# A block product of the output done by seven smaller products, GpSimd's work in short pieces, and loads asked for one stage ahead

## The chip, the cores and the metric

The kernel runs on one core of a Trainium2 chip. The core has TensorE (PE, matrix products; PEld is its weight load), VectorE (DVE), ScalarE (ACT), GpSimd (POOL) and the queue of SyncE (SP), from which nearly all transfers are issued. Every engine works through its own list of instructions in order, and semaphores make one engine wait for another. The metric is the device time of one execution in microseconds (us), as the median of several runs.

## The reference

Two stages follow each other. The first is an attention without a softmax over pairs: q is normalised along the head's 64 elements, k along the sequence, and a 64x64 product of k and v for each batch and head is applied to q. The second is a two-layer network with an exact Gelu over all tokens.

```
q_s = exp(q - max) / sum over d          # [8, 8, 576, 64]
k_s = exp(k - max) / sum over s
kv  = einsum('bhsd,bhse->bhde', k_s, v)
x   = einsum('bhsd,bhde->bhse', q_s, kv) -> [4608 tokens, 512]
h   = x @ w_in                           # 512 -> 2048
g   = 0.5 * h * (1 + erf(h / sqrt(2)))
out = g @ w_out                          # 2048 -> 512
```

## The kernel before

The tokens go through in nine chunks of 512. Chunk c = 0 to 7 holds the first 512 positions of batch c; chunk 8 (`B` in the code) holds the remaining 64 positions of all eight batches. All matrix operands are bf16, sums are f32 in the eight banks of PSUM.

**The stages of a chunk.** In the steady part (chunks 3 to 7) TensorE's order is: the first layer of chunk c (`h_waves`), the second layer of chunk c (`y_phase`), and, ahead of that layer's last product, `next_x`: the x of chunk c+1 (`x_all`), the transposing DMA of q for batch c+2 (`xbar_step`), and the k-v product of batch c+2 (`kv_step`). So attention runs two batches ahead of the network's output. The order of everything is written out by hand: the kernel's text is the order on each engine, and a layer beneath it adds the semaphores. `y_phase` takes a table `ins` of functions, and `after(i)` calls those of entry i at that place.

**Seven products instead of eight.** Both layers are 2x2 block products, done with seven products of half size and sums of their operands and results. In the second layer the blocks are 256 tokens by 1024 by 256 columns. Product m is 16 matmuls with a stationary 128x128 block and 256 moving columns (`mm` in `y_phase`, line 691). Product 3 multiplies g[UP, LO], the upper half of g's 1024 rows for the first 256 tokens, by the upper right block of the weights, in which a difference of weights was stored before. Its result goes to the bank `bx` (named yx) and from there to the output's block `c12`. The products' order is 4, 3, 5, 1, 2, 6, then `next_x`, then 7. Products 5, 1 and 2 use sums that VectorE makes in `s_parts` (arrays s5 and s12); 6 and 7 use differences that it makes in place in g (lines 404 and 405).

**Around the change.** At the end of `h_waves` the Gelus of the last quarter tiles (lines 606 and 607) and `s_parts` run on ScalarE and VectorE while TensorE is already in the output phase. In `y_phase`, ScalarE then copies yd (line 706), takes the exponentials of q for batch c+2 (entry 8: a table load and four activations), copies yx (709), takes those of k (entry 9) and copies the second yd (724). VectorE subtracts (716), makes the row sums of q (`q_sums`, in entry 1), and combines results (719, 721, 731). GpSimd first makes a one-element copy that depends on the last in-place difference (`touch_g`, 1086), casts v to bf16 in four pieces (line 190), scales q in one instruction of 2048 elements a partition (`q_scale`, 269), and does the two last combinations of the output on 128x512 f32 tiles (732 and 733). Only then SP can send the first of the two output stores.

**Loads.** `load(nb)` asks for q, k and v of batch nb from SP at the start of chunk c = nb-2's first layer; `load_qrest` does so for chunk 8's q. Each of the three has two buffers. Batches 2 to 4 are loaded earlier. The transposing DMA and the output stores are on the same queue.

In `h_waves`, VectorE's sums that are written r (`r_sum`) and qb (`e_sum`) take a PSUM bank and an SBUF tile or the reverse; TensorE's product 7 of the first layer may write the bank qa only after `e_sum` has read it. `x_sums` makes the operand sums of the first layer (quad_t).

The functions that the change touches, with their callers:

Of the kernel before, what the change touches and what calls it, by code (L numbers as in the profile page):

```python
# [16 lines left out]
def kernel(  # L17
# [70 lines left out]
    HT = M // 2  # L88
    HN = DM // 2
    w7 = singles.tile([128, HK, HN], BF16)  # L90
    s12 = singles.tile([128, HK, M], BF16)
    s5 = singles.tile([128, HK, HT], BF16)

# [10 lines left out]
    def load_main(b, name, t, parts=1):  # L104
# [5 lines left out]
        for i in range(parts):  # L110
            nc.sync.dma_start(out=f[:, i * n:(i + 1) * n, :], in_=src[:, i * n:(i + 1) * n, :])

    def load_pair(b, name, t, parts=1):
        f = f32in.tile([128, HP, NS * D], FP32, tag=name + "f")
        st[b][name + "f"] = f
        src = t[b].rearrange("h (p n) d -> (h p) (n d)", n=NS).rearrange("(x q) f -> q x f", q=128)
        n = HP // parts
        for i in range(parts):
            h0 = i * n
            if b == 0 and name == "k" and i == 0:  # L120

                nc.scalar.dma_start(out=f[:, 0, :], in_=src[:, 0, :])
                h0 = 1
            nc.sync.dma_start(out=f[:, h0:(i + 1) * n, :], in_=src[:, h0:(i + 1) * n, :])
# [8 lines left out]
    def load_v1(i):  # L133

        if i == 0:
            st[1]["vf"] = f32in.tile([128, HP, NS * D], FP32, tag="vf", name="f")
        src = v[1].rearrange("h (p n) d -> (h p) (n d)", n=NS)
        nc.sync.dma_start(out=st[1]["vf"][:, i, :], in_=src[i * 128:(i + 1) * 128, :])

# [52 lines left out]
    def cast_v_all(b):  # L192
        for hp in range(HP):
            cast_v(b, hp, nc.gpsimd)
# [71 lines left out]
    def q_scale(b, eng, i=0, n=1):  # L266
        w = H // n
        e = st[b]["eq"][:, :, i * w:(i + 1) * w, :]
        eng.tensor_tensor(  # L269
            out=e, in0=e, in1=st[b]["recq"].unsqueeze(3).to_broadcast([128, J, w, D]), op=ALU.mult,  # L270
        )

    def norm_q(b, i=0, n=1, eng=None):

# [184 lines left out]
        roles.update(bb=r["x3"], ba=r["kv1"], x0=r["bb"], x1=r["kv0"], x2=r["x0"], x3=r["ba"],  # L459
                     kv0=r["x1"], kv1=r["x2"])  # L460

    def h_waves(c, mid):

# [48 lines left out]
        def r_sum(q):  # L514
            tt(held["r", q], held["A", q], held["r", q])
# [49 lines left out]
        else:  # L565
# [11 lines left out]
            mm(7, 0, 1)  # L577
            r_sum(0)
            r_sum(1)
            mm(3, 0, 1)  # L580
            for q in (2, 3):
                mm(5, q)
# [22 lines left out]
            mm(4, 2, 3)  # L605
        gelu("A", 2, 3)
        gelu("B", 2, 3)
        s_parts(c, 0, 4, (0,))
        if mid:
            s_parts(c, 0, 4, (4,))  # L610
        s_parts(c, 0, 4, (2,))
        s_parts(c, 4, 4, (0,))
        s_parts(c, 4, 4, (3,))
        s_parts(c, 4, 4, (4,))
        turn_roles()
# [54 lines left out]
        }  # L670
        return act, wgt

    def y_phase(c, ins):

# [23 lines left out]
        def after(i):  # L700
            for fn in ins.get(i, []):
                fn()

        mm(4, bd, True)
        if c > 1:
            nc.scalar.copy(out=f, in_=bd)
            after(8)
            mm(3, bx, True)
            nc.scalar.copy(out=c12, in_=two(bx))
            after(9)  # L710
        else:
            nc.vector.tensor_copy(out=f, in_=bd)
        after(0)
        mm(5, be, True)
        after(7)
        tt(f, f, be, ALU.subtract)
# [9 lines left out]
        if c == 1:  # L726
            mm(3, be, False)
            nc.scalar.copy(out=c12, in_=two(be))
        after(4)
        mm(6, bb, True)  # L730
        tt(c22, c22, two(bb))
        tt(c22, c22, c12, eng=nc.gpsimd)
        tt(c22, c22, c21, ALU.subtract, eng=nc.gpsimd)
        after(5)
        mm(7, ba, False)
        tt(c11, two(f), two(ba))
        y_store(c, 1, ysb[1])
        y_store(c, 0, ysb[0])
        after(6)

    def y_last(c):

# [304 lines left out]
    for t in range(4):  # L1047
# [4 lines left out]
    mix_wo(1, 1)  # L1052
    mix_wo(3, 1)
    quad["r"] = wst.tile([128, 4, 2, HT], FP32, tag="w2", name="r")
    quad["t"] = wst.tile([128, 4, 2, HT], BF16, tag="w3", name="quad_t")
    h1 = {p + 3: [lambda p=p: cast_v(2, p, nc.scalar)] for p in range(HP)}
    h1[1] = [sums[0]]
    h1[3] += sums[1:3]
# [3 lines left out]
    exp_q(2, parts=2)  # L1062
    exp_k(2)

    y_phase(1, {
        0: [sums[3]],
        7: [lambda: norm_q(2, 0, 2)],
        1: [lambda: norm_q(2, 1, 2, nc.vector)],
        2: [lambda: cast_v_all(3), lambda: xbar_step(2), lambda: exp_q(3)],
        3: [lambda: kv_step(2), lambda: exp_k(3), lambda: q_sums(3)],  # L1070
        4: [lambda: table(AF.Gelu)],
        6: [lambda: load(4), lambda: x_all(2, (3, 4, 1, 5)),
            lambda: kv_step(3, lambda: x_sums(2, (1,))), lambda: x_sums(2, (2,))],
    })

    def q_late():


        nc.gpsimd.tensor_copy(out=scr[:, 2:3], in_=quad["r"][:, 0, 0, 0:1])
        q_scale(3, nc.gpsimd)  # L1080
        xbar_step(3)

    def touch_g(c):

# [13 lines left out]

    for c in range(2, B + 1):
        nb = c + 2  # L1100
        if 2 < c and nb < B:
            load(nb)
        elif nb == B:
            load_qrest()
        h_waves(c, q_late if c == 2 else None)
        s_parts(c, 4, 4, (2,))
        yi = {}
        if nb <= B:
            yi[8] = [lambda: exp_q(nb)]
            yi[1] = [lambda: norm_q(nb)]  # L1110
            yi[3] = [lambda: table(AF.Gelu)]
        if nb < B:
            yi[9] = [lambda: exp_k(nb)]
            yi[0] = [lambda: touch_g(c), lambda: cast_v_all(nb)]
        if c < B:
            yi[5] = [lambda: next_x(c, nb)]
            y_phase(c, yi)
        else:
            y_last(c)

# [29 lines left out]
```

## Time and profile before

| | us |
|---|---|
| median of 3 runs | 256.49 |
| lowest and highest | 256.13, 256.66 |
| the profiled execution's own time | 256.13 |
| its span on the engines | 254.3 |
| one steady chunk (product 4 at 136.48 to 162.23) | 25.75 |
| TensorE busy | 247.7 |
| VectorE, ScalarE, GpSimd busy | 209.0, 189.1, 67.3 |

The span is what the profile draws, from the first instruction to the last; the run's own time has 1.8 us more around it. A row of a timeline gives the start in us from the span's start, the length in us, the engine, the source line, the operation, output and inputs by the program's names, sizes, and the count that was merged into the row; in brackets stands how long the engine was idle before it and what ended that. Source lines can be those of a helper: 428 is the helper of all tensor-tensor sums, 497 and 694 the matmuls of the two layers. A matmul's length includes its way through the array; the next one starts long before it ends.

### The profile page before, as it was taken

To read this page: it belongs to the slowest core of one execution; us is meant where nothing else is said; L and a number is where in the kernel's file an instruction comes from. 1 tells how busy PE (TensorE), PEld (TensorE's weight loads), DVE (VectorE), ACT (ScalarE), POOL (GpSimd) and SP (SyncE) were. 2 spreads that over 40 slices of the span, in tenths; PEclk is the share of its full clock that TensorE was granted. 3 is DMA by queue.
4 is the path that set the end of the run, shared out by engine and by line. 5 is a ranking of instruction groups with operands and counts; after the bars stand their busy time and mean duration, and the time that the engine had idled before them with its cause. 6 is when DMAs were issued, how large, how long until landed. Compare 5 with 4: busy or idle time off the path is not lost.

```text
span 254.3 us, 6526 instructions
## 1 busy us (share of the span) xinstructions
PE 247.7 (97%) x2672; PEld 195.8 (77%) x2678; DVE 209.0 (82%) x365; ACT 189.1 (74%) x321; POOL 67.3 (26%) x64
## 2 busy tenths in 40 slices
PE   7899999999999999999999999999999999999994
PEld 3444444448888888888888888888888888888883
DVE  1878799888986989897889888988898889578972
ACT  4785988699977995899689968896886787158711
POOL 1530023000735067006700580059000900040000
PEclk9999999999999999999999999999999999999999
DMA  7999999994439935980499049904830340012033
GB/s 237 400 387 425 402 406 400 398 411 174 85 125 330 266 68 131 321 340 1 109 303 377 4 85 326 378 0 86 263 71 0 84 166 3 0 55 115 1 82 86
DMA packets 43166, 50.23 MB, mean 198 GB/s; under 512 B 20224, under 2 KB 30464, under 8 KB 42880
## 3 DMA queue, kind: packets, MB, share of 16 engines
q1 hardware_dynamic: 42416, 49.13, 57.7%
q10 hardware_dynamic: 720, 0.69, 1.0%
q8 instruction: 21, 0.34, 0.6%
q14 instruction: 9, 0.07, 0.1%
HBM read 36.70 MB, written 9.44 MB: 181 GB/s over the span
## 4 chain that ended last, share of the span: by engine, by line
PE 93%; DMA 4%; ACTq 0%; issue 0%; DVE 0%; POOL 0%
PE qa L497 19%; PE ps L377 11%; PE ya L694 10%; PE qb L497 10%; PE yd L694 10%; PE ye L694 6%; PE ps L637 5%; PE qc L497 5%; PE yb L694 5%; PE yx L694 4%; PE kv L225 2%; DMA touch<-in_moe_w_in_dram 2%; DMA f<-in_v_dram 2%; PE ps L343 2%; PE ya L764 1%; PE yd L764 1%
## 5 line engine op out<-in xcount | busy, mean ns | idle before, releaser
L497 PEld LDWEIGHTS <-quad_s 128*128 128x128 bf16 x448 | 43.8, 98 | 5.3 <-issue 0.2
L694 PEld LDWEIGHTS <-g 128*128 128x128 bf16 x448 | 43.2, 98 | 5.8 <-issue 0.4
L269 POOL TENSOR_TENSOR e<-e,recq 128x2048 bf16<-128x2048 bf16 (+1 forms) x9 | 27.4, 3046 | 72.9 <-DVE recq L264 47.7
L694 PEld LDWEIGHTS <-s 128*128 128x128 bf16 x336 | 32.9, 98 | 3.8
L497 PEld LDWEIGHTS <-wi_bf 128*128 128x128 bf16 x336 | 32.8, 98 | 3.9
L497 PE MATMUL qa<-quad_t,quad_s 128*128 128x256 bf16 x224 | 29.4, 272 | 0.0
L377 PE MATMUL ps<-xT,wi_bf 128*128 128x512 bf16 x124 | 27.8, 379 | 0.2
L428 POOL TENSOR_TENSOR y_sb<-y_sb 128x512 f32<-128x512 f32 x14 | 19.5, 1390 | 24.2 <-DVE y_sb L428 21.3
L263 DVE TENSOR_REDUCE qsum<-e 128x16 f32<-128x1024 bf16 (+1 forms) x12 | 20.9, 1743 | 4.8 <-ACT e L173 4.8
L377 PEld LDWEIGHTS <-wi_bf 128*128 128x128 bf16 x128 | 12.3, 97 | 15.2 <-issue 0.5
L428 DVE TENSOR_TENSOR qb<-qa,r 128x512 f32<-128x512 f32 x28 | 18.1, 694 | 5.8 <-ACT g L521 3.1
L505 ACT COPY qc<-qa 128x512 f32<-128x512 f32 x26 | 13.9, 577 | 12.0 <-PE qa L497 11.5
L383 ACT ACTIVATE g<-ps 128x512 bf16<-128x512 f32 x32 | 17.6, 603 | 6.1 <-PE ps L377 5.8
L173 ACT ACTIVATE e<-f 128x512 bf16<-128x512 f32 (+1 forms) x42 | 20.5, 556 | 1.9 <-DMA f<-in_q_dram 1.8
L521 ACT ACTIVATE g<-r 128x512 bf16<-128x512 f32 x28 | 17.3, 631 | 6.2 <-DVE r L428 6.2
L521 ACT ACTIVATE g<-qc 128x512 bf16<-128x512 f32 x28 | 15.2, 594 | 7.7 <-PE qc L497 7.7
L428 DVE TENSOR_TENSOR r<-qa,r 128x512 f32<-128x512 f32 x28 | 18.0, 685 | 0.9 <-PE qa L497 0.7
L402 DVE TENSOR_TENSOR s<-g 128x1024 bf16<-128x1024 bf16 x28 | 18.6, 686 | 0.0
L190 POOL CAST v_aug<-f 128x576 bf16<-128x576 f32 x25 | 17.2, 723 | 3.6 <-DMA f<-in_v_dram 3.6
L178 ACT ACTIVATE ek<-f 128x2304 bf16<-128x2304 f32 (+1 forms) x10 | 17.3, 1735 | 0.5 <-DMA f<-in_k_dram 0.5
L521 ACT ACTIVATE g<-qb 128x512 bf16<-128x512 f32 x28 | 15.1, 594 | 0.7 <-PE qb L497 0.7
L497 PE MATMUL qb<-quad_t,quad_s 128*128 128x256 bf16 x112 | 15.5, 272 | 0.0
(101 smaller groups left out, 469.3 us busy)
## 6 DMA issues: line engine op xcount, KB each, us to landing
out_dram<-y_sb SPq DMA_DIRECT2D x16, 512.0 KB, 3.4
f<-in_k_dram SPq DMA_DIRECT2D x6, 1152.0 KB, 10.0
f<-in_v_dram SPq DMA_DIRECT2D x6, 1152.0 KB, 11.7
f<-in_q_dram SPq DMA_DIRECT2D x6, 1024.0 KB, 8.1
w<-in_moe_w_in_dram SPq DMA_DIRECT2D x6, 512.0 KB, 8.7
f<-in_v_dram SPq DMA_DIRECT2D x8, 288.0 KB, 6.3
f<-in_q_dram SPq DMA_DIRECT2D x4, 512.0 KB, 8.9
w<-in_moe_w_out_dram SPq DMA_DIRECT2D x2, 1024.0 KB, 12.3
```

The lines of the kernel that those rows point to most:

```text
L173: nc.scalar.activation(out=dst[:, i], in_=src[:, u], func=AF.Exp)
L178: nc.scalar.activation(out=ek[b % 2][:, i:i + n], in_=st[b]["kf"][:, i:i + n].rearrange("p x (n d) -> p x n d", n=NS), func=AF.Exp,)
L190: eng.tensor_copy(out=o, in_=i)
L263: nc.vector.reduce_sum(out=qsum, in_=st[b]["eq"][:, :, i * w:(i + 1) * w, :], axis=AX.X)
L269: eng.tensor_tensor(out=e, in0=e, in1=st[b]["recq"].unsqueeze(3).to_broadcast([128, J, w, D]), op=ALU.mult,)
L377: nc.tensor.matmul(ps, wi_bf[:, dm, t * 128:(t + 1) * 128], st[c]["xT"][:, dm, :], start=(dm == 0), stop=(dm == NDM - 1),)
L383: nc.scalar.activation(out=st[c]["g"][:, t, :], in_=ps, func=AF.Gelu)
L402: tt(out=s12[:, a, half], in0=g[:, a, half], in1=g[:, b, hi], op=ALU.add)
L428: eng.tensor_tensor(out=out, in0=in0, in1=in1, op=op)
L497: nc.tensor.matmul(held[kind, q][:, u], w, mov[m][:, k], start=(m in (1, 5) and u == 0 and k == 0), stop=(k == 1), skip_group_check=True,)
L521: nc.scalar.activation(out=g[:, t:t + 2, half], in_=held[kind, q], func=AF.Gelu)
L694: nc.tensor.matmul(ps[:, j * HN:(j + 1) * HN], act[m][:, k, j * 128:(j + 1) * 128], wgt[m][:, k, :], start=(first and k == 0 and j == 0), ...
```

## The change

Product 3 is itself done as a 2x2 block product by seven products of blocks of 128 tokens, 512 and 128 columns, in the output phases of chunks 3 to 7. Chunk 2's and 8's are as before. A class `Two` holds it:

- `weights`: five sums of weight blocks, made once by GpSimd: two in output phase 1, three and a change of sign in chunk 2.
- `sums`: sums of blocks of g for `rows`, `diag` and `cols`, made by VectorE, half of them after `r_sum(1)` and half after `r_sum(3)` in `h_waves`.
- `mm`: four matmuls with 128 moving columns for each small product. Products 4, 5 and 1 of the small ones go first, before the large product 4; products 2, 3, 6 and 7 take the place of the large product 3. All go to four quarters of the bank bx.
- `snap`: between the two, ScalarE copies three quarters of the bank (384 columns) to the tile `two_d`.
- `corner`, `corner2`, `spread`: six sums of 128x128 f32 on GpSimd, with which the snapshot completes the two diagonal quarters of c12.

Beside that, GpSimd's scaling of q becomes eight instructions of 256 elements (`q_scale_parts`), its two combinations of 128x512 become eight of 128x128, and three of the four casts of v move behind `corner2`. `load(nb + 1)`, or `load_qrest`, is now called in entry 1 of `y_phase`, after the scaling of q, instead of `load(nb)` at the chunk's start. v has a buffer by name (`v_buf`): batches 4 and later share one, and the other one's place is taken by the tile of `Two` after batch 3. Entries 4 and 6 of `y_phase` changed places, and entry 10 stands where 4 was.

```diff
+    def v_buf(b):
+        i = b % 2 if b < 4 else 0
+        return f32in.tile([128, HP, NS * D], FP32, tag=f"vf{i}", name="f", bufs=1)
...
+    def q_scale_parts(b):
+        for j in range(J):
+            for i in (0, 4):
+                e = st[b]["eq"][:, j, i:i + 4, :]
+                nc.gpsimd.tensor_tensor(
+                    out=e, in0=e, op=ALU.mult,
+                    in1=st[b]["recq"][:, j, i:i + 4].unsqueeze(2).to_broadcast([128, 4, D]),
+                )
...
             r_sum(0)
             r_sum(1)
+            if sums:
+                sums(c, 0)
             mm(3, 0, 1)
...
         gelu("B", 2, 3)
-        s_parts(c, 0, 4, (0,))
-        if mid:
-            s_parts(c, 0, 4, (4,))
-        s_parts(c, 0, 4, (2,))
-        s_parts(c, 4, 4, (0,))
+        if sums:
+            sums(c, 1)
+        else:
...
+    class Two:
+        def weights(self, part):
+            W = wo_bf[:, UP, HN:DM].rearrange("p (a h b) n -> p h a b n", h=2, b=2)
...
+        def sums(self, c, a):
+            A = st[c]["g"][:, UP, LO]
+            k, k1, k2 = slice(4 * a, 4 * a + 4), slice(4 * a, 4 * a + 2), slice(4 * a + 2, 4 * a + 4)
+            o = slice(2 * a, 2 * a + 2)
+            lo, hi = slice(0, 128), slice(128, HT)
+            tt(self.rows[:, o], A[:, k1], A[:, k2])
+            tt(self.diag[:, o], A[:, k1, lo], A[:, k2, hi])
+            if a:
+                s_parts(c, 0, 4, (0,))
+            tt(self.cols[:, k], A[:, k, hi], A[:, k, lo], ALU.subtract)
+            if a:
+                s_parts(c, 4, 4, (0,))
+                s_parts(c, 0, 4, (2,))
+        def mm(self, c, ps, sets, first):
+            A, W = st[c]["g"][:, UP, LO], wo_bf[:, UP, HN:DM]
+            lo, hi = slice(0, 128), slice(128, HT)
+            for m in sets:
+                for i, k1 in enumerate((0, 1, 4, 5)):
+                    k2 = k1 + 2
+                    lhs, rhs, r = {
+                        1: (self.diag[:, i], self.w[:, 0, i], 0),
+                        2: (self.rows[:, i, hi], W[:, k1, lo], 2),
+                        3: (A[:, k1, lo], self.w[:, 1, i], 1),
+                        4: (A[:, k2, hi], self.w[:, 2, i], 2),
+                        5: (self.rows[:, i, lo], W[:, k2, hi], 1),
+                        6: (self.cols[:, k1], self.w[:, 3, i], 3),
+                        7: (self.cols[:, k2], self.w[:, 4, i], 0),
+                    }[m]
...
+        def snap(self, ps):
+            nc.scalar.copy(out=two_d, in_=ps[:, 0:384])
+        def corner(self):
+            eng, d = nc.gpsimd, self.d
+            tt(d[:, 2], d[:, 2], d[:, 1], ALU.subtract, eng=eng)
+            tt(d[:, 0], d[:, 0], d[:, 2], eng=eng)
+        def corner2(self, o):
+            eng, d = nc.gpsimd, self.d
+            tt(d[:, 0], d[:, 0], o[:, 0, 128:HN], eng=eng)
+            tt(d[:, 0], d[:, 0], o[:, 1, 0:128], ALU.subtract, eng=eng)
+        def spread(self, o):
+            tt(o[:, 0, 0:128], o[:, 0, 0:128], self.d[:, 2], eng=nc.gpsimd)
+            tt(o[:, 1, 128:HN], o[:, 1, 128:HN], self.d[:, 0], eng=nc.gpsimd)
...
+        if p3:
+            p3.mm(c, bx, (4, 5, 1), True)
+            p3.snap(bx)
         mm(4, bd, True)
         if c > 1:
             nc.scalar.copy(out=f, in_=bd)
             after(8)
-            mm(3, bx, True)
+            if p3:
+                p3.mm(c, bx, (2, 3, 6, 7), False)
+            else:
+                mm(3, bx, True)
             nc.scalar.copy(out=c12, in_=two(bx))
             after(9)
...
         after(0)
+        if p3:
+            p3.corner2(c12)
+        after(6)
         mm(5, be, True)
...
-        tt(c22, c22, c12, eng=nc.gpsimd)
-        tt(c22, c22, c21, ALU.subtract, eng=nc.gpsimd)
+        if p3:
+            p3.spread(c12)
+        for x, op in ((c12, ALU.add), (c21, ALU.subtract)):
+            for j in range(2):
+                for n in (slice(0, 128), slice(128, HN)):
+                    tt(c22[:, j, n], c22[:, j, n], x[:, j, n], op, eng=nc.gpsimd)
...
-        if 2 < c and nb < B:
-            load(nb)
-        elif nb == B:
-            load_qrest()
-        h_waves(c, q_late if c == 2 else None)
+        p3 = y3 if 2 < c < B else None
+        h_waves(c, q_late if c == 2 else None, p3 and p3.sums)
...
-            yi[1] = [lambda: norm_q(nb)]
+            yi[1] = [lambda: q_sums(nb), lambda: q_scale_parts(nb)]
             yi[3] = [lambda: table(AF.Gelu)]
+        if nb + 1 < B:
+            yi[1].append(lambda: load(nb + 1))
+        elif nb + 1 == B:
+            yi[1].append(load_qrest)
         if nb < B:
             yi[9] = [lambda: exp_k(nb)]
-            yi[0] = [lambda: touch_g(c), lambda: cast_v_all(nb)]
+            cv = [lambda hp=hp: cast_v(nb, hp, nc.gpsimd) for hp in range(HP)]
+            yi[0] = [lambda: touch_g(c)] + ([p3.corner] if p3 else []) + cv[:1]
+            yi[6] = cv[1:]
+        elif p3:
+            yi[0] = [p3.corner]
```

## The prediction

> **What bounds the kernel now.** I read the busy shares and the clock first, then the chain that ended last, and then, for one chunk in the steady part, the timelines of the engines around the place that is changed.
>
> ```profile
> PE 247.7 (97%) x2672; PEld 195.8 (77%) x2678; DVE 209.0 (82%) x365; ACT 189.1 (74%) x321; POOL 67.3 (26%) x64
> PEclk9999999999999999999999999999999999999999
> PE 93%; DMA 4%; ACTq 0%; issue 0%; DVE 0%; POOL 0%
> ```
>
> TensorE is the bound: 93% of the chain, at the full granted clock, and the list of waits, asked for TensorE between 110 and 226 us, is empty. So only two things can move the time: fewer TensorE columns, or a new TensorE wait. In order of time, the chain shows what product 3 (yx) costs in one chunk:
>
> ```profile
> 136.48 1.75 PE yd L694 x16
> 138.22 1.75 PE yx L694 x16
> 139.97 1.75 PE ye L694 x16
> ```
>
> The timeline gives the pace of single matmuls. A group lasts from its first start to its last end, so the pace is the group less one matmul (272 ns for 256 columns, 219 ns for 128, in the tile view), over one less than the count.
>
> ```profile
> 138.06 1.91 PE L694 MATMUL yx<-wo_bf,g 128*128 128x256 bf16 x16
> ...
> 153.33 1.04 PE L497 MATMUL qa<-quad_t,quad_s 128*128 128x256 bf16 x8
> ...
> 204.21 1.19 PE L497 MATMUL qa<-quad_t,quad_s 128*128 128x256 bf16 x8
> ...
> 249.57 0.99 PEld L764 LDWEIGHTS <-g 128*128 128x128 bf16 x16
> 249.68 1.06 PE L764 MATMUL ya<-w,g 128*128 128x128 bf16 x16
> ```
>
> 256 columns: (1.91-0.27)/15 = 0.109 us. 128 columns, each with its own weight load: (1.06-0.22)/15 = 0.056 us. The row at 204.21 is one small wait that is there today: 1.19 where the same eight take 1.04, so 0.15 us, at the opening of chunk 7.
>
> **The change, part by part.** *Product 3.* Sixteen matmuls at 0.109 (1.75 us) become 28 at 0.056 (1.57 us): 0.18 us less in each of five chunks, 0.90 us in all, wholly on the path.
>
> *The snapshot.* TensorE now does 12 small matmuls (0.67 us), product 4 (1.75), then the other 16 small ones, into the same bank. These must wait until ScalarE has copied the bank's first 384 columns. ScalarE around that place:
>
> ```profile
> 135.16 1.23 ACT L521 ACTIVATE g<-r 128x512 bf16<-128x512 f32 x2 [0.56 <-DVE r L428]
> 136.30 1.06 ACT L521 ACTIVATE g<-qa 128x512 bf16<-128x512 f32 x2
> 137.25 1.08 ACT L521 ACTIVATE g<-qb 128x512 bf16<-128x512 f32 x2
> 138.26 0.59 ACT L706 COPY zeros<-yd 128x512 f32<-128x512 f32 x1
> 138.86 1.28 ACT L173 ACT_TABLE_LOAD   x1
> ```
>
> The output phase starts on TensorE at 136.31. ScalarE is on its Gelus without a pause until about 138.23, where the snapshot goes. Copies of 256 columns take 0.37 to 0.42 us, of 512 0.59; for 384 I take 0.49, midway, so it ends at 138.72. A ScalarE cast that ended at 11.181 released a matmul at 11.232, so 0.05 more: 138.77. TensorE gets there at 136.31+0.67+1.75 = 138.73. The wait is 0.04 us a chunk (0 with the shortest copy, 0.14 with the longest): +0.2 us for five. Queued behind the snapshot on ScalarE: the copy of yd, which now waits for product 4's end (138.93, 0.67 later), the table load, the exponentials of q, the copy of yx. VectorE's row sums of q follow them, at 143.1 instead of 142.43; VectorE is idle 0.76 us before it takes yb at 146.99, and that absorbs it. The bank of ye, which the x products reuse, is then read by 146.3, and TensorE wants it at 146.7.
>
> *VectorE's operand sums*: four of 128x512 bf16 and two of 128x256. Rows of the same kind are 0.41 and 0.29 us, the next one starting 0.33 and 0.20 after: 1.7 us a chunk, in two halves. The first goes in after the r sums:
>
> ```profile
> 128.22 1.29 DVE L428 TENSOR_TENSOR r<-qa,r 128x512 f32<-128x512 f32 x2
> 129.96 0.69 DVE L509 COPY r<-qb 128x512 f32<-128x512 f32 x1 [0.46 <-PE qb L497]
> 130.84 0.69 DVE L509 COPY r<-qb 128x512 f32<-128x512 f32 x1 [0.18 <-PE qb L497]
> 131.44 0.68 DVE L402 TENSOR_TENSOR s<-g 128x1024 bf16<-128x1024 bf16 x1
> 132.64 1.30 DVE L428 TENSOR_TENSOR qb<-qa,r 128x512 f32<-128x512 f32 x2 [0.51 <-ACT g L521]
> ```
>
> The half takes 0.87 us; from 129.42 it ends at 130.29, the copies at 131.5, the s sum at 132.1, and the qb sums start at 132.64 as before. 0.54 us stay spare there, and TensorE's product 7 asks for the second qb sum 0.15 us after it is done. The second half starts at 135.64: rows ready at 136.06 (needed at 136.53), diagonal at 136.27 (needed at 136.76). The s and g sums behind it end at 141.7 instead of 140.66; products 5, 1 and 2 read theirs after 139.7, and the g ones come last. Nothing.
>
> *GpSimd.* Today it does 9 us a chunk, with two long stretches:
>
> ```profile
> 145.23 3.62 POOL L269 TENSOR_TENSOR e<-e,recq 128x2048 bf16<-128x2048 bf16 x1 [1.81 <-ACT ek L178]
> 148.81 2.94 POOL L428 TENSOR_TENSOR y_sb<-y_sb 128x512 f32<-128x512 f32 x2
> ...
> 200.31 2.95 POOL L428 TENSOR_TENSOR y_sb<-y_sb 128x512 f32<-128x512 f32 x2
> ```
>
> The 1024 and 2048 forms of e (1.90, 3.62) give 1.68 ns an element and some 0.14 between starts beyond it, so an eighth is 0.57: 4.5 us for eight. Alone, the 128x512 f32 row takes 1.27; a quarter lies between 0.32 (no fixed cost) and 0.62 (all that exceeds 1.68 ns an element is fixed). I take 0.41, the fixed 0.14 with the rest by size: that split also fits the casts of 256 and 576 (0.41, 0.67). New order after 141.9: two corner pieces, one cast, a wait for the yx copy (143.5), two pieces, three casts (146.3; the kv products need them after 147.2, so 0.9 us of cover), eight e pieces (150.9), ten y_sb pieces: 155.0, some 155.7 with VectorE in between. It ended at 151.75. The next chunk's first operand sums are at 155.3: this is the thin place, taken as nothing in the sum, and as a rival below.
>
> What pieces may give: VectorE's two-input sums from SBUF stand still while GpSimd runs one.
>
> ```profile
> 200.82 1.31 DVE L428 TENSOR_TENSOR quad_t<-xT,quad_t 128x512 bf16<-128x512 bf16 x1
> ```
>
> Alone this takes 0.41; here it ends 0.28 after the first y_sb at 201.85. That delay leads to the 0.15 us wait at 204.21. With pieces it waits one piece at most, so I take the 0.15 back: between 0 and 0.15.
>
> *The loads.* SP sends two stores, q and k of the next batch, v (which now waits for GpSimd's casts, 146.3, since v has one buffer), then the transposing DMA, then stores. Behind v's wait is only the transpose, whose own data is ready at 150.9. Were v to take its present 11.7 us to land, and the transpose 3.9 after that, qT is there at 163, and its product reads it at 172.6. v is wanted at 166. No TensorE wait on a load exists today, so nothing is gained: 0. The stores go 4 us later, land by 159.5, and their buffer is next written at 168.
>
> *Once only.* Two weight sums in output phase 1, about 1.0 us each, fill 2.38 us in which GpSimd waits; with pieces the store and load(4) go 0.7 us later, and v of batch 4 still lands 1.1 us ahead of its cast. Four more behind the e row of 76.66 run to about 84.3, where GpSimd then idles until 90.43; VectorE's s sum at 83.92 may wait 0.4, and the operand in that row of work that is needed first (product 5's second half, 88.7) is done at 87.7. 0.
>
> **Sum**: -0.90 + 0.20 - 0.15 = -0.85 us. The profiled execution took 256.13 (span 254.3 and 1.8 around it), the fastest of the three shown; the median is 256.49. 255.3 on the first, 255.6 on the second: I say 255.4.
>
> **Rivals.** *A, the snapshot eats it (no change).* Against the 0.18 a chunk stands a wait of 0.14 with a 512-column copy, 0.18 if ScalarE is 0.04 later still. Net 0 to -0.35 with the opening wait: 255.8 to 256.1. For it: the path to 138.72 has no slack at all. Chance 0.22.
>
> *B, GpSimd's tail meets the operand sums (slower).* With quarter pieces of 0.62, GpSimd goes on to 157.3, and rows, diagonal and cols, issued from 155.3, each wait for a piece: up to 1.5 us late where 0.69 is spare, so up to 0.8 us at product 7 in chunks 4 to 7, and 0.45 where only part of it collides: 4 x 0.45 = 1.8, so 257.1. It decides from 0.22 us a chunk. For it: the row at 200.82. Against: by my piece the tail is 0.4 us into the sums. The Trainium skill, "SBUF — State Buffer", section "Who interferes with whom", says that the pair of ports goes to whoever is first for its whole instruction, the other fully blocked; the row at 200.82 agrees (0.9 us of standstill). By that rule more pieces mean more such meetings, each shorter. Chance 0.17.
>
> *C, small matmuls go at the pace of their weight loads (slower).* A weight load takes 97 to 98 ns; were the 28 paced by that, 28 x 0.098 = 2.74 us, +1.0 a chunk: 260.3. Against it stand the 16 at 249.68, at 0.056 with loads overlapped (0.99 us for 16). Chance 0.04. The Trainium skill, "TensorE: Matmul & The Clock Gate", section "Back-to-back issue gap", gives about 81 ns a matmul of 128 columns for sustained pairs of load and matmul; by an estimate from that figure five chunks would be 2.6 us slower, and the row at 249.68 does not bear it out.
>
> **How the numbers follow.** About 0.2% (0.5 us) is what a measurement here can tell from no change. My case 0.53, A 0.22, B 0.17, C 0.04, anything else 0.04. Faster: my case and a little of the rest, 0.54. Same: A and the mild end of B, 0.25. Slower: 0.21. Low: all 1.05 us gained, and 0.15 of scatter, 254.9. High: through A and the lower half of B, 256.9; what is left out is C, the upper half of B and some of the rest.
>
> **What would show it.** 28 matmuls of yx at 0.056 in chunks 3 to 7; a gap of 0.04 us before the 13th (A: 0.15 or more); GpSimd's last y_sb piece near 155.7 of this chunk's clock, with VectorE's qb sums still starting when TensorE's product 6 ends (B: later, with a TensorE wait in product 7); no wait at the opening of chunk 7; the chain over 90% TensorE. I am wrong if TensorE's list of waits in the steady part is no longer empty by more than 0.1 us a chunk.

## The result, and the profile after

The changed kernel takes 255.62 us (median of 20 runs, 255.21 to 256.40), the kernel before on the same chip 256.44 (20 runs, 256.02 to 257.06). The ratio is 0.9967 with a 95% interval of 0.9959 to 0.9975: 0.8 us or 0.33% faster. 255.4 was forecast.

The busy shares, the granted clock and the engines' shares of the chain, from the page of the changed kernel:

```profile
PE 247.9 (98%) x2738; PEld 196.1 (77%) x2738; DVE 219.1 (86%) x395; ACT 190.4 (75%) x326; POOL 102.8 (40%) x177
PEclk9999999999999999999999999999999999999998
PE 81%; DMA 16%; DVE 1%; SPq 0%; issue 0%
```

TensorE is still the bound, and the list of its waits between 80 and 226 us is still empty. (That list leaves out short waits: the runs below lose up to 0.25 us at one place without an entry in it. The small waits below are read from the starts of the matmuls.) GpSimd went from 67.3 to 102.8 us, VectorE from 209.0 to 219.1; neither sets the end. TensorE holds a smaller share of this chain than of the one before only because the chain here was followed back through the opening's loads instead of through TensorE; the prediction's sign of over 90% was missed for that reason.

A profiled execution has some scatter in that opening, which is bound by loads: the first product of the output starts between 57.7 and 58.4 us in the runs below, before any added instruction (GpSimd's first weight sum is at 68.9). So I compare the **steady stretch**, from TensorE's start of chunk 3's output phase to its start of chunk 8's: five changed chunks and nothing of the opening. Before it lasts from 110.51 to 238.32, 127.82 us; after from 110.95 to 237.91, 126.97 us. That is 0.85 less, the sum of the prediction. The starts, before and after:

```profile
110.51 1.91 PE L694 MATMUL yd<-wo_bf,g 128*128 128x256 bf16 x16
238.32 1.04 PE L764 MATMUL yd<-wo_bf,g 128*128 128x256 bf16 x8
```
```profile
110.95 0.39 PE L753 MATMUL yx<-two,g 128*128 128x128 bf16 x4
237.91 1.04 PE L882 MATMUL yd<-wo_bf,g 128*128 128x256 bf16 x8
```

The spans differ by 0.4 alone, because this execution lost 0.44 in the opening. Each stretch is from one execution. How far it can be trusted shows in the stage ahead of it, from chunk 2's output phase to chunk 3's, in which no edit changes TensorE's work: it takes 25.81 us in all fourteen profiled executions, within 0.01. The run times also hold the opening and the last stores, and differ from the stretch by up to 0.6 us.

The chain of the changed kernel in order of time (start, length, engine, tile, line, count), for two chunks:

```profile
136.75 0.67 PE yx L753 x12
137.42 1.75 PE yd L799 x16
139.17 0.92 PE yx L753 x16
...
162.35 0.67 PE yx L753 x12
163.02 1.75 PE yd L799 x16
164.76 0.97 PE yx L753 x16
```

Twelve small matmuls take 0.67, 0.056 each. The other sixteen, with their wait for the snapshot, take 0.92 to 0.97 where 0.90 would be bare. The large product 3 took 1.75 in their place.

### The profile page after: what moved, and what is told of

It is laid out like the page before. It is cut to its first block, busy times and chain, and to the rows that moved or that the text cites. A ratio compares the mean times of both kernels' runs of the same rounds, so it can differ in the third digit from the quotient of the medians.

```text
span 253.9 us, 6825 instructions
## 1 busy us (share of the span) xinstructions
PE 247.9 (98%) x2738; PEld 196.1 (77%) x2738; DVE 219.1 (86%) x395; ACT 190.4 (75%) x326; POOL 102.8 (40%) x177
## 4 chain that ended last, share of the span: by engine, by line
PE 81%; DMA 16%; DVE 1%; SPq 0%; issue 0%
PE qa L513 19%; PE ya L799 10%; PE qb L513 10%; PE yd L799 10%; DMA f<-in_q_dram 7%; PE ye L799 6%; PE ps L393 6%; PE yb L799 5%; PE qc L513 5%; DMA w<-in_moe_w_out_dram 3%; DMA w<-in_moe_w_in_dram 3%; PE yx L753 3%; DMA f<-in_v_dram 2%; PE kv L231 2%; PE ps L359 1%; PE ya L882 1%
## 5 line engine op out<-in xcount | busy, mean ns | idle before, releaser
L799 PEld LDWEIGHTS <-g 128*128 128x128 bf16 x368 | 35.2, 98 | 4.8 <-issue 0.4
L275 POOL TENSOR_TENSOR e<-e,recq 128x1024 bf16<-128x1024 bf16 (+1 forms) x4 | 9.3, 2330 | 47.8 <-DVE recq L270 41.0
L444 POOL TENSOR_TENSOR y_sb<-y_sb 128x128 f32<-128x128 f32 x56 | 26.0, 498 | 2.8 <-issue 2.8
L284 POOL TENSOR_TENSOR e<-e,recq 128x256 bf16<-128x256 bf16 x40 | 24.7, 653 | 1.8 <-DVE recq L270 1.2
L418 DVE TENSOR_TENSOR s<-g 128x1024 bf16<-128x1024 bf16 x28 | 19.8, 726 | 0.0
L1213 POOL CAST scr<-g 128x1 f32<-128x1 bf16 x4 | 0.7, 187 | 42.3 <-DVE g L421 42.3
```

The lines of the kernel that those rows point to most:

```text
L284: nc.gpsimd.tensor_tensor(out=e, in0=e, op=ALU.mult, in1=st[b]["recq"][:, j, i:i + 4].unsqueeze(2).to_broadcast([128, 4, D]),)
L418: tt(out=s12[:, a, half], in0=g[:, a, half], in1=g[:, b, hi], op=ALU.add)
L444: eng.tensor_tensor(out=out, in0=in0, in1=in1, op=op)
L799: nc.tensor.matmul(ps[:, j * HN:(j + 1) * HN], act[m][:, k, j * 128:(j + 1) * 128], wgt[m][:, k, :], start=(first and k == 0 and j == 0), ...
```

## The experiments

Every ratio is against the kernel before on the same chip (medians 256.34, 256.35 and 256.19 us in the three groups of runs). The steady stretch is from the profiled execution of each kernel. All diffs are against the changed kernel.

### The three parts one at a time

Small products alone: the loads are asked for at the chunk's start and GpSimd's long operations stay long.

```diff
-        for x, op in ((c12, ALU.add), (c21, ALU.subtract)):
-            for j in range(2):
...
+        tt(c22, c22, c12, eng=nc.gpsimd)
+        tt(c22, c22, c21, ALU.subtract, eng=nc.gpsimd)
...
+        if 2 < c and nb < B:
+            load(nb)
+        elif nb == B:
+            load_qrest()
...
-            yi[1] = [lambda: q_sums(nb), lambda: q_scale_parts(nb)]
+            yi[1] = [lambda: norm_q(nb)]
...
-        if nb + 1 < B:
-            yi[1].append(lambda: load(nb + 1))
-        elif nb + 1 == B:
-            yi[1].append(load_qrest)
```

> Product 3 by seven small products alone: GpSimd's scaling of q and its two last combinations in one instruction each, and the loads at the start of the chunk, as in the kernel before. I read the steady stretch, from the start of chunk 3's output phase to that of chunk 8 on TensorE: 127.81 us before, 126.96 after. Theory (the columns of product 3 carry the gain): 18 hundredths a chunk less and a snapshot wait of 0.02 to 0.08, so about 127.15 to 127.25, with a wait of 0.15 or a little more at the opening of chunk 7, since the long combinations on GpSimd still hold up VectorE's operand sums and now start later. Rival (the gain comes from the pieces and the loads): 127.8, no gain.

Measured: 257.65 us, ratio 1.0058 (1.0045 to 1.0072), steady stretch 129.42. The expectation failed. The part that saves the matmuls makes the kernel slower when it stands alone: with 0.90 saved on TensorE and 1.60 lost in sum, 2.5 us of new waits. VectorE, GpSimd and TensorE of this kernel at the turn from chunk 4 to chunk 5, by their timelines:

```profile
149.36 2.04 DVE L444 TENSOR_TENSOR quad_t<-xT 128x512 bf16<-128x512 bf16 x1
...
151.51 0.29 DVE L252 TENSOR_TENSOR kvc<-kv,rec 128x128 bf16<-128x128 f32 x1
```
```profile
147.50 3.62 POOL L275 TENSOR_TENSOR e<-e,recq 128x2048 bf16<-128x2048 bf16 x1
...
152.20 2.88 POOL L444 TENSOR_TENSOR y_sb<-y_sb 128x512 f32<-128x512 f32 x2
```
```profile
151.86 1.05 PE L513 MATMUL qb<-quad_t,quad_s 128*128 128x256 bf16 x8 [0.56 <-DVE kvc L252]
```

The scaling of q (e) starts at 147.50 instead of 145.23 (this chunk itself began 0.58 later), since GpSimd now has the corner sums ahead of it, and in this chunk also waited 0.42 for v. So it still runs when VectorE comes to the first quad_t at 149.36. That sum takes 2.04 instead of 0.42 and ends 0.28 after e does. The reciprocals and the scaling of the k-v products (kvc) are queued behind it. TensorE's product 5 (qb) reads this quad_t, and it writes the bank from which the first kvc row reads. That row ends at 151.80, and the group starts at 151.86, 0.72 late against the pace of 0.87 for eight (0.56 of it shown as idle). Product 5 waits like that in chunks 4 to 6 (0.19, 0.72, 0.24); in chunk 7, which has no kvc row ahead of it, it does not. Product 7 of the first layer waits 0.12 and 0.16 in chunks 4 to 6, and 0.38 and 0.16 in chunk 7, where the long y_sb sums meet the operand sums.

The Trainium skill, "SBUF — State Buffer", section "Who interferes with whom", lets a VectorE instruction with two SBUF inputs contend with a GpSimd instruction that reads SBUF, for an exclusive lock. The row at 149.36 agrees: 1.6 us of standstill until e was over.

Pieces alone, without the small products (and with the loads at the chunk's start):

```diff
-        2: [lambda: cast_v_all(3), first_weights, lambda: xbar_step(2), lambda: exp_q(3)],
+        2: [lambda: cast_v_all(3), lambda: xbar_step(2), lambda: exp_q(3)],
...
-        y3.weights(1)
...
-        p3 = y3 if 2 < c < B else None
+        p3 = None
+        if 2 < c and nb < B:
+            load(nb)
+        elif nb == B:
+            load_qrest()
...
-        if nb + 1 < B:
-            yi[1].append(lambda: load(nb + 1))
-        elif nb + 1 == B:
-            yi[1].append(load_qrest)
```

> Product 3 in one, loads at the start of the chunk, and only GpSimd's scaling of q and its two combinations in pieces. Theory: the 0.15 us wait at the opening of chunk 7 goes, nothing else: steady stretch 127.65, time 0.15 us less than before, which the runs can hardly tell. Rival (pieces carry the gain): 127.2 or less.

Measured: 256.48 us, ratio 1.0003 (0.9994 to 1.0013), steady stretch 127.65. The wait of 0.15 at the opening of chunk 7 is gone, nothing else changed.

Early loads alone, without the small products and their weight sums, and with GpSimd's long operations (the combinations as in the first diff):

```diff
-        p3 = y3 if 2 < c < B else None
+        p3 = None
...
-            yi[1] = [lambda: q_sums(nb), lambda: q_scale_parts(nb)]
+            yi[1] = [lambda: norm_q(nb)]
```

> Product 3 in one, GpSimd in long instructions, only the loads asked for one stage ahead (and one buffer for v from batch 4 on). Theory: no TensorE wait hangs on a load, so the steady stretch stays at 127.8 within 0.05. Rival (earlier loads shorten the stage): 127.6 or less. A loss would show as a wait of the k-v product on GpSimd's casts.

Measured: 256.46 us, ratio 1.0005 (0.9996 to 1.0014), steady stretch 127.81 against 127.82 before. Worth nothing alone.

### Which pieces matter

The scaling of q in one instruction, all else as changed:

```diff
-            yi[1] = [lambda: q_sums(nb), lambda: q_scale_parts(nb)]
+            yi[1] = [lambda: norm_q(nb)]
```

> The changed kernel with GpSimd's scaling of q in one instruction of 2048 elements again, everything else as changed. New theory after the run of product 3 alone (one long GpSimd instruction, started later because GpSimd first waits for the copy of yx, now lies across VectorE's first operand sum quad_t and holds it until it ends): e runs from about 146.7 to 150.3 of chunk 4's clock, quad_t comes 0.6 to 0.8 us late, TensorE waits at product 5 in chunks 4 to 6; no 0.1 to 0.2 us waits in product 7. Steady stretch 128.2 to 128.6 (126.96 with all pieces). Rival (the cost in the run of product 3 alone came from the loads at the chunk's start): 127.0.

Measured: 257.11 us, ratio 1.0029 (1.0017 to 1.0041), steady stretch 128.03: 1.06 us worse than the changed kernel, in waits of 0.18 to 0.23 at product 5 and 0.13 more behind it in chunks 4 to 6. That is a little below the expected 128.2 to 128.6.

The two combinations of 128x512 f32 as one instruction each, q's scaling still in pieces:

```diff
-        for x, op in ((c12, ALU.add), (c21, ALU.subtract)):
-            for j in range(2):
...
+        tt(c22, c22, c12, eng=nc.gpsimd)
+        tt(c22, c22, c21, ALU.subtract, eng=nc.gpsimd)
```

> The changed kernel with GpSimd's two last combinations of 128x512 in one instruction each again, the scaling of q in pieces. New theory: product 5 waits no more, but the later operand sums of quad_t are held up, so product 7 of the first layer waits 0.1 to 0.3 us in chunks 4 to 7: steady stretch 127.4 to 128.1. Rival (only the scaling of q matters): 127.0.

Measured: 255.79 us, ratio 0.9976 (0.9965 to 0.9987), steady stretch 126.86. The expectation failed: it is 0.1 us shorter than the changed kernel, not half a microsecond longer. GpSimd and VectorE of this kernel:

```profile
152.82 2.69 POOL L444 TENSOR_TENSOR y_sb<-y_sb 128x512 f32<-128x512 f32 x2
```
```profile
155.50 0.41 DVE L444 TENSOR_TENSOR two<-g 128x512 bf16<-128x512 bf16 x1
155.83 0.28 DVE L444 TENSOR_TENSOR quad_t<-g 128x256 bf16<-128x256 bf16 x1
156.04 0.41 DVE L444 TENSOR_TENSOR two<-g 128x512 bf16<-128x512 bf16 x1
```

And the same place in the changed kernel, GpSimd and then VectorE:

```profile
146.71 4.97 POOL L284 TENSOR_TENSOR e<-e,recq 128x256 bf16<-128x256 bf16 x8
151.64 1.05 POOL L444 TENSOR_TENSOR y_sb<-y_sb,two_d 128x128 f32<-128x128 f32 x2
152.65 3.71 POOL L444 TENSOR_TENSOR y_sb<-y_sb 128x128 f32<-128x128 f32 x8
```
```profile
155.33 0.72 DVE L444 TENSOR_TENSOR two<-g 128x512 bf16<-128x512 bf16 x1
155.97 0.54 DVE L444 TENSOR_TENSOR quad_t<-g 128x256 bf16<-128x256 bf16 x1
156.44 0.41 DVE L444 TENSOR_TENSOR two<-g 128x512 bf16<-128x512 bf16 x1
156.77 1.27 DVE L525 COPY r<-qb 128x512 f32<-128x512 f32 x2
```

Eight pieces take 3.71 us, two long ones 2.69. The pieces run until 156.36, into the operand sums that begin at 155.33, and hold the first two of them (0.72 and 0.54 instead of 0.41 and 0.28). The long ones are over at 155.51, just as the sums begin. Short pieces make each meeting shorter and the tail longer; here the tail decides. It costs TensorE the 0.1 us, by a way that the prediction did not follow. In chunks 5 and 6 of the changed kernel VectorE then runs without a pause into the qb sums and begins them 0.05 late. The r sums, the Gelus on ScalarE and the snapshot come 0.05 later with them, and the 16 small matmuls take 0.97 with their wait. With the long combinations VectorE pauses 0.34 ahead of the same sums, and they take 0.92 and 0.91. The qb sums of chunk 6 in the changed kernel, then the same and chunk 5's matmuls in this one:

```profile
184.22 1.28 DVE L444 TENSOR_TENSOR qb<-qa,r 128x512 f32<-128x512 f32 x2
```
```profile
184.17 1.30 DVE L444 TENSOR_TENSOR qb<-qa,r 128x512 f32<-128x512 f32 x2 [0.34 <-issue]
```
```profile
164.83 0.92 PE yx L753 x16
```

Both long, the loads early:

```diff
-        for x, op in ((c12, ALU.add), (c21, ALU.subtract)):
-            for j in range(2):
...
+        tt(c22, c22, c12, eng=nc.gpsimd)
+        tt(c22, c22, c21, ALU.subtract, eng=nc.gpsimd)
...
-            yi[1] = [lambda: q_sums(nb), lambda: q_scale_parts(nb)]
+            yi[1] = [lambda: norm_q(nb)]
```

> The changed kernel with both of GpSimd's long works in long instructions again (scaling of q, the two combinations), early loads kept: the fourth corner of a table, beside all as changed (126.97), pieces with late loads (133.38) and long instructions with late loads (129.42). Theory (two causes: long instructions hold up quad_t; late loads hold up GpSimd's first cast and what is queued behind it): with early loads only the first is left, 127.9 to 128.4, as with the long scaling alone (128.03). Rival (long instructions alone make all of the 129.42): 129.4.

Measured: 257.65 us, ratio 1.0055 (1.0041 to 1.0069), steady stretch 129.01, beyond what was expected. Product 5 waits 0.20 to 0.25, and product 7 has its 0.13 and 0.16 again, in chunk 7 0.37 and 0.16. So the long combinations cost nothing (-0.1) while q's scaling is in pieces and 1.0 us (129.01 - 128.03) while it is long. One long instruction makes VectorE's list late enough that the next one meets something. In chunk 7's opening, where half of the 1.0 us lies, an operand sum starts at 203.58, just behind the first long combination (203.46), and takes 1.43 us. With q's scaling in pieces the same sum starts at 202.36, ahead of the long combinations at 203.40, and takes 0.65.

### The loads

Loads at the chunk's start, all else as changed:

```diff
+        if 2 < c and nb < B:
+            load(nb)
+        elif nb == B:
+            load_qrest()
...
-        if nb + 1 < B:
-            yi[1].append(lambda: load(nb + 1))
-        elif nb + 1 == B:
-            yi[1].append(load_qrest)
```

> The changed kernel with the loads of batches 5 to 7 and of chunk 8's q at the start of the chunk again; pieces and small products as changed. Theory (no wait hangs on a load): steady stretch 126.97 within 0.1, time as the changed kernel. Rival (early loads are needed beside product 3, since GpSimd's first cast and its tail are tighter): waits of GpSimd's first cast on v, of the k-v product, 127.2 or more.

Measured: 261.96 us, ratio 1.0225 (1.0194 to 1.0256), steady stretch 133.38. My theory (no difference) failed, and the rival held, though the cost of 6.4 us is far above the 0.2 that it named as its least. The way of it runs over four engines. SP's queue, then GpSimd, VectorE and TensorE of this kernel:

```profile
130.41 0.83 SPq L677 DMA_DIRECT2D out_dram<-y_sb  x2
131.28 0.79 SPq L112 DMA_DIRECT2D f<-in_q_dram  x1
132.11 1.44 SPq L130 DMA_DIRECT2D f<-in_k_dram  x1
133.66 0.74 SPq L130 DMA_DIRECT2D f<-in_v_dram  x1
```
```profile
146.03 0.66 POOL L196 CAST v_aug<-f 128x576 bf16<-128x576 f32 x1 [3.21 <-DMA f<-in_v_dram]
146.65 0.98 POOL L444 TENSOR_TENSOR two_d<-two_d,y_sb 128x128 f32<-128x128 f32 x2
```
```profile
147.67 0.69 DVE L444 TENSOR_TENSOR y_sb<-y_sb,ye 128x512 f32<-128x512 f32 x1 [2.05 <-POOL two_d L444]
```
```profile
148.41 0.62 PE L359 MATMUL ps<-qT,kvc 64*64 64x512 bf16 x7 [1.55 <-DVE y_sb L444]
```

The stores wait for GpSimd's last combination, which now ends 4.4 us later (they left SP at 125.97 before), and the loads are queued behind the stores. v lands at about 146. GpSimd's first cast stands still 3.21 us for it, `corner2` is queued behind the cast, VectorE's sum of y_sb and ye waits for `corner2` (2.05 idle), and TensorE's x product waits 1.55 for the bank that this sum reads. Then the clock falls. The view by windows (window; its length; busy time of PE, PEld, DVE, ACT and POOL; granted clock, DMA share, GB/s):

```profile
146.00:148.00 2.00, 0.86 (x6) 0.33 (x5) 0.33 (x1) 1.39 (x2) 1.89 (x4) 1.00 0.00 0
148.00:149.90 1.90, 1.35 (x79) 1.14 (x78) 1.80 (x4) 1.05 (x2) 1.90 (x4) 1.00 0.00 0
149.90:151.60 1.70, 1.70 (x19) 1.25 (x10) 1.67 (x5) 0.02 (x1) 1.70 (x4) 0.56 0.04 10
151.60:153.30 1.70, 1.70 (x10) 1.21 (x9) 1.15 (x4) 0.00 (x0) 1.70 (x4) 0.50 0.00 0
153.30:155.00 1.70, 1.70 (x17) 1.46 (x16) 1.26 (x2) 0.97 (x3) 1.70 (x4) 0.94 0.00 0
```

For 3.4 us after the wait TensorE runs at about half clock (0.56 and 0.50); a product of 16 matmuls then takes 3.46 us instead of 1.9. Half of 3.4 us is 1.7 us lost, about as much again as the wait itself. The Trainium skill, "TensorE: Matmul & The Clock Gate", section "What's actually happening", has the clock halved after an idle window of about 3.4 us and full again after a busy one. The halving and the 3.4 us agree; the stop that came before was only 1.55 us here, though TensorE was busy for no more than 2.21 of the 3.90 us between 146 and 149.9 (0.86 and 1.35).

To separate GpSimd's queue from the late data, the same late loads with all four casts behind `corner2`:

```diff
-            yi[0] = [lambda: touch_g(c)] + ([p3.corner] if p3 else []) + cv[:1]
-            yi[6] = cv[1:]
+            yi[0] = [lambda: touch_g(c)] + ([p3.corner] if p3 else cv[:1])
+            yi[6] = cv if p3 else cv[1:]
...
+        if 2 < c and nb < B:
+            load(nb)
+        elif nb == B:
+            load_qrest()
...
-        if nb + 1 < B:
-            yi[1].append(lambda: load(nb + 1))
-        elif nb + 1 == B:
-            yi[1].append(load_qrest)
```

> The kernel with pieces and late loads (133.38), but all four casts of v behind the two sums corner2, so that a late v no longer holds up corner2, and with it VectorE's sum of yx and ye, the bank of ye and TensorE's x product. Theory (the late v costs mostly through the queue on GpSimd): the x product waits no more; v lands at about 146 of chunk 4's clock, the casts end near 148.5 where the k-v product wants them from 147.3, so a wait of 0.5 to 1.2 us moves there in chunks 4 and 5: steady stretch 128.5 to 131. Rival (the late v itself is the whole cost, wherever the cast stands): 133 or more.

Measured: 260.06 us, ratio 1.0160 (1.0139 to 1.0181), steady stretch 131.08: 2.3 us of the 6.4 come back, and it ends 0.08 above the expected range. The x product no longer waits in chunk 4; the k-v products do (0.17 and 0.60). The clock stays full, and the time from chunk 4's output phase to chunk 5's falls from 29.63 to 26.61; the other chunks are no shorter. A later load is late too. ScalarE and VectorE of this kernel, chunk 6:

```profile
194.98 1.28 ACT L179 ACT_TABLE_LOAD   x1 [1.44 <-DMA f<-in_q_dram]
196.28 2.19 ACT L179 ACTIVATE e<-f 128x512 bf16<-128x512 f32 x4
```
```profile
198.50 2.29 DVE L269 TENSOR_REDUCE qsum<-e 128x32 f32<-128x2048 bf16 x1 [1.43 <-ACT e L179]
...
201.09 0.63 DVE L444 TENSOR_TENSOR y_sb<-y_sb,ye 128x512 f32<-128x512 f32 x1
```

Here it is chunk 8's q that comes late: the table load waits 1.44 for it, the row sums of q 1.43 for the exponentials, and the sum at 201.09, for whose bank TensorE waits 0.52, is queued behind them. So in both kernels the stores' later departure does the damage, through whichever load is behind them.

### The snapshot

The snapshot twice:

```diff
             nc.scalar.copy(out=two_d, in_=ps[:, 0:384])
+            nc.scalar.copy(out=two_d, in_=ps[:, 0:384])
```

> The changed kernel with the snapshot copy made twice, one after the other (a copy of 384 columns starts about 0.40 us after the one ahead of it). Theory (the snapshot's end is what TensorE waits for, with no slack): the wait ahead of the second set of small products grows from 0.02 to 0.08 to 0.42 to 0.48 us in each of five chunks: steady stretch 126.96 + 2.0 = 129.0, slower than before by 1.2. Rival (TensorE's gap there has another cause, the change from 256 to 128 columns for one): 126.96, unchanged.

Measured: 257.87 us, ratio 1.0064 (1.0052 to 1.0077), steady stretch 129.43. ScalarE and TensorE of this kernel:

```profile
139.01 0.50 ACT L761 COPY two_d<-yx 128x384 f32<-128x384 f32 x1
139.54 0.48 ACT L762 COPY two_d<-yx 128x384 f32<-128x384 f32 x1
```
```profile
140.07 0.38 PE L753 MATMUL yx<-wo_bf,two 128*128 128x128 bf16 x4 [0.38 <-ACT two_d L762]
```

The second copy starts 0.53 behind the first (0.40 was expected), and the five chunks are 2.46 us longer, 0.49 each. All but 0.04 of what is added to ScalarE at that place comes out at the end: as the prediction said, the path to the snapshot has no slack.

The other direction: the first twelve small matmuls and the snapshot ahead of ScalarE's last Gelu, and the VectorE sums that they need ahead of the rest.

```diff
-        gelu("B", 2, 3)
+        gelu("B", 2)
+        def ahead():
+            y3.bx = bank(roles["x0"], "yx")
+            y3.mm(c, y3.bx, (4, 5, 1), True)
+            y3.snap(y3.bx)
+            gelu("B", 3)
...
-        if p3:
-            p3.mm(c, bx, (4, 5, 1), True)
-            p3.snap(bx)
```

> The changed kernel with the first three small products asked for, and the snapshot made, ahead of ScalarE's last Gelu of the chunk instead of behind it. Theory (TensorE waits 0.02 to 0.08 us a chunk for the snapshot, 0.23 in all): the snapshot ends 0.5 us sooner, the wait goes, steady stretch 126.74, no other wait, since the Gelu that moves behind it is read about 1 us later. Rival (the gap is the price of going from 256 to 128 columns): 126.97. A loss would mean that the late Gelu holds up VectorE.

Measured: 255.40 us (255.30 to 255.78), ratio 0.9967 (0.9956 to 0.9978), steady stretch 126.77: 0.20 less than the changed kernel, and no TensorE wait at the snapshot. ScalarE of this kernel has the copy between the last two Gelus:

```profile
137.66 0.49 ACT L770 COPY two_d<-yx 128x384 f32<-128x384 f32 x1
138.02 0.63 ACT L537 ACTIVATE g<-qb 128x512 bf16<-128x512 f32 x1
```

With the two long combinations of the earlier experiment as well (both diffs together):

> The snapshot ahead of ScalarE's last Gelu, and GpSimd's two combinations of 128x512 in one instruction each: both left-over costs that the changed kernel has. Theory: the combinations in one go end GpSimd's tail 0.6 us sooner, the operand sums of product 3 meet no GpSimd work; no snapshot wait: 126.75, and 255.4 us or a little less. Rival (they do not add up, the long combinations hold up quad_t once the rest is earlier): 126.9 or more.

Measured: 255.42 us (255.34 to 255.56), ratio 0.9968 (0.9956 to 0.9981), steady stretch 126.74. That is the shortest stretch of all, 1.08 below the kernel before. But in the run times neither version can be told from the changed kernel's ratio of 0.9967.

### GpSimd's tail made longer

Six more sums of 128x128 f32 at the end of GpSimd's work in each chunk, into a part of `two_d` that nothing reads any more:

```diff
+        if p3:
+            for i in range(6):
+                tt(p3.d[:, 1], p3.d[:, 2], p3.d[:, 0], eng=nc.gpsimd)
```

> The changed kernel with six more sums of 128x128 f32 on GpSimd behind its last combination in chunks 3 to 7 (into a tile that nobody reads), so that its tail ends about 2.5 us later. Theory (the tail meets VectorE's operand sums, of whose 0.69 us of room 0.57 are used): VectorE's sums for rows, diag, cols and the s sum behind them each wait for a piece, 0.3 to 0.6 us more in all; waits at product 7 of 0.2 to 0.5 us in chunks 4 to 7: steady stretch 127.8 to 129. Rival (VectorE slips in between the pieces without loss): 127.0.

Measured: 257.27 us, ratio 1.0043 (1.0028 to 1.0058), steady stretch 128.65, inside what was expected. GpSimd, VectorE and TensorE of this kernel:

```profile
156.37 3.56 POOL L444 TENSOR_TENSOR two_d<-two_d 128x128 f32<-128x128 f32 x6
```
```profile
156.48 0.67 DVE L444 TENSOR_TENSOR two<-g 128x512 bf16<-128x512 bf16 x1
...
158.27 0.81 DVE L418 TENSOR_TENSOR s<-g 128x1024 bf16<-128x1024 bf16 x1
```
```profile
159.74 1.19 PE L513 MATMUL qa<-quad_t,quad_s 128*128 128x256 bf16 x8
```

With GpSimd at work until 159.9, all three operand sums and the s sum behind them are held. TensorE's product 7 starts at 159.74, 0.2 late, and its row is 0.15 long beyond 1.04. In four chunks such waits make up 1.4 of the 1.68 us, and the snapshot, at 0.13 in each of them, the rest. This is the price of rival B, close to its 0.45 a chunk.

## Why the prediction was right

The steady stretch carries the whole gain, and its terms came out close to the sum; in two of them errors of about 0.1 us cancelled.

- **Small matmuls, -0.90.** 0.056 us each, as the row with 16 of them at the end of the kernel before had shown: right. Rival C is refuted by the changed kernel itself. So is the rate of about 81 ns that the Trainium skill, "TensorE: Matmul & The Clock Gate", section "Back-to-back issue gap", gives for sustained pairs: 12 took 0.67 us, each with its own weight load. Rival C's price was added up 0.9 us too low: the gain of 0.18 a chunk falls away with it, so it is 256.1 + 5.0 and not 255.3 + 5.0. Nothing hangs on that.
- **The snapshot, +0.20.** The waits are 0.02, 0.02, 0.08, 0.08 and 0.03 us: 0.23. The copy of 384 columns took 0.50 where 0.49 was interpolated. That the total fits so well is luck in part: with the long combinations the waits are 0.03 at most and 0.13 in all, and the other 0.10 belongs to GpSimd's tail, which the sum put at nothing. Moving the copy took 0.20 off, doubling it added 0.49 a chunk. Rival A had the right place and the wrong size.
- **The opening of chunk 7, -0.15.** Gone; pieces alone take it away (-0.17) and early loads alone do not.
- **GpSimd's tail, 0.** It cost 0.1 us. The pieces were sized right: an f32 piece took 0.45 and the next started 0.41 after it, an e piece 0.615 and 0.57. Those that met a VectorE sum took about 0.2 longer. The eight combinations took 3.71, and the tail ended at 156.4 instead of 155.7 (0.3 of that is this execution's later start of the chunk). It cost VectorE 0.57 us, more than the 0.54 that were spare ahead of the qb sums. The prediction counted another 0.15 behind them, up to TensorE's product 7, and there nothing waits. But the Gelus and the snapshot also hang on these sums, and in chunks 5 and 6 the snapshot came 0.05 later; with the long combinations it did not. At product 7 rival B stayed off by 0.12 us, and six more pieces brought it.
- **The loads and the pieces.** Here the working was too thin, although the sum was right. It priced early loads at "nothing is gained: 0", and the pieces at "between 0 and 0.15", each against the kernel before. Both prices hold there: 127.81 and 127.65 against 127.82. But the small products make GpSimd's work longer, and without the other two parts that turns into waits: small products with neither are 1.6 us slower than the kernel before. The prediction saw the link itself ("The stores go 4 us later") and did not follow what is queued behind those stores when the loads stay at the chunk's start.

The steady stretch with and without the small products, in us:

| | GpSimd in pieces | GpSimd long |
|---|---|---|
| small products, loads early | 126.97 | 129.01 |
| small products, loads at the chunk's start | 133.38 | 129.42 |
| no small products, loads early | not run | 127.81 |
| no small products, loads at the chunk's start | 127.65 | 127.82 (before) |

Beside the small products pieces are worth 2.0 us, provided that the loads are early; early loads are worth 6.4 with pieces and 0.4 without. Pieces with late loads are worse than long operations with late loads by 4.0: they make the tail longer, and the stores leave later with the loads behind them. The parts do not add up, and no single one of them is measurably faster than the kernel before in the run times.

Of the 6.4 us, 4.0 lie in the period with the halved clock (29.63 against 25.59); the clock fell nowhere else in the steady stretch of that run. Still open are the small waits that make up the rest, which were not followed one by one.

## What to carry to other kernels

Price each part of a change twice: against the kernel before, and with the other parts taken as done. A part that is worth nothing alone may be the cover of another. When work is added to an engine that is off the path, follow its last instruction to what is queued behind it on each queue, the loads behind a store above all. Cut long GpSimd operations where VectorE's two-input sums meet them, and leave them long where nothing does: pieces cost more in total.

## What the runs showed of the hardware

- A VectorE sum with two SBUF inputs took 2.04 us instead of 0.42 when it met one GpSimd instruction of 3.62 us.
- Two sums of 128x512 f32 on GpSimd took 2.69 us, the same work in eight pieces 3.71.
- After a stop of 1.55 us and some thin work, TensorE's granted clock was half for 3.4 us (about 150.1 to 153.5), so the loss was about twice the wait.
